# First loads in pieces, idle transposes at the start, reciprocals behind the next maxima

## The chip, the cores and the metric

The kernel runs on one core of one Trainium2 chip. The metric is the device time of the program in microseconds (us), taken as the median of several runs; beside it there is one execution under the hardware profiler, from which every row of the trace comes. The engines are named PE (TensorE), DVE (VectorE), ACT (ScalarE), POOL (GpSimd) and SP (SyncE, which here only issues DMAs). PEld is PE's weight load.

## The reference

Attention with pooled queries, then two feed-forward layers. All data are float32.

```python
q_pool = q.reshape(B, H, S // 2, 2, D).mean(axis=3)      # B 2, H 8, S 1152, D 64
scores = matmul(q_pool, k.T) / sqrt(D)                   # 576 queries x 1152 keys, 16 heads
attn = exp(scores - max(scores))
attn = attn / (sum(attn) + 1e-09)
x = matmul(attn, v)                                      # then (B * 576) x 512
h = x @ w_in;  g = maximum(h, 0) + log1p(exp(-abs(h)));  x = g @ w_out       # 512 -> 2048 -> 512
xn = x / sqrt(mean(x * x) + 1e-06) * rms_g
g = xn @ w_gate;  x = (g / (1 + exp(-g))) * (xn @ w_val) @ w_out2            # 512 -> 1536 -> 512
```

## The kernel before

**Stages.** Attention takes some 290 us, the two feed-forward layers the rest. Attention goes over 8 pairs of heads (`pb`), and within a pair over 4 blocks of 128 queries (`x` 0 to 3) for each head `h`, and a fifth, `x` 4, which holds the last 64 queries of both heads.

**Preparation of a pair (`prep`).** A float32 operand is split into a rounded part and the rest, which PE multiplies one after the other. The keys of both heads come as one tile `kr` (576 KB); for each head `kk` gets the rounded keys on one half of the partitions (a copy, L251 or L253, called at L369) and the rest on the other half (a subtraction, L256, called at L371). The queries come as `qr`, twice for each head (the same 288 KB into either half of the partitions), are summed in pairs into `qs` (L256, called at L353), and scaled and rounded into `qh` (L381 or L383) with the rest in `ql` (L363); 512 columns for the first four blocks, and 64 for the tail. For the first pair the query loads are issued on ACT's queue, all else on SP's. `v` is loaded as it is. `prep(0)` stands first; `prep(1)` follows the first scores; `prep(pb + 1)` is called in block 1 of pair `pb`.

**A block.** `qk` (L400) puts 128 x 1152 scores into PSUM with 6 matmuls (3 for `qh`, 3 for `ql`; 12 in the fifth block). `softmax` takes the negated maximum on DVE (`nm`, L416) and the exponential on ACT (`p`, L418), which also adds up the row sums in `den`. `flip` (L437; `flip_m`, L681, for the fifth block) transposes `p` on PE through two small PSUM banks `t`, with copies to `pt` on ACT or DVE; `av` (L455) multiplies by `v` with 36 matmuls.

**End of a pair.** `scales` works on DVE: add 1e-9 to the 9 columns of `den` (L466), reciprocal (L468), and two copies that repeat it over 64 columns a head (`rdb`, L469 with 512 columns and L472 with 128). `spread` transposes `rdb` on PE (L488) during blocks 1 and 2 of the next pair and multiplies the result of the pair by it.

**The order.** A planner (`Plan`) knows the operations, their engines with estimated durations, and the tiles that they read and write. PE's order is that of the program: in the last block of a pair the transposes, the scores of the next pair's first block (head 1 in block 3, head 0 in block 4), `av`, and then the transposes of the next pair's first block. The order on DVE, ACT, POOL and SP comes out of a list schedule by the latest start that each operation could have; where an operation names two engines, the planner takes one. In its model a POOL operation and a DVE operation that uses the port to SBUF exclude each other in time.

## Time and profile before

| | us |
|---|---|
| time, median of 3 runs (lowest to highest) | 717.67 (717.59 to 718.02) |
| profiled execution: time | 715.96 |
| profiled execution: span from the first to the last instruction | 714.2 |
| busy PE / DVE / ACT / POOL | 681.2 / 447.5 / 334.6 / 100.2 |

The profiled execution's time is 1.76 us longer than its span. Start and end times in rows are microseconds from the start of the span. A wait that a row names is put down to the event that came last.

### The profile page before, as it was taken

The page shows a single profiled execution, that of the slowest core. Times are in us where ns is not written, and L with a number is a line of the kernel's source. Part 1 is how long each engine was busy: PE and PEld are TensorE (multiplying, and loading weights), DVE is VectorE, ACT ScalarE, POOL GpSimd, SP SyncE. Part 2 cuts the span into 40 slices and gives each one's busy share as a digit, 9 for nine tenths or more (in the row PEclk, how much of TensorE's full clock was granted, in tenths as well). Part 3 has the DMA queues.
Part 4 walks back from the last instruction along what each step waited for, and adds up shares of the span by engine and source line. Part 5 has one row for each costly group of instructions (what it writes and reads, how often), then busy time and mean ns, then how long its engine had stood idle before and what let it go on. Part 6 is the DMA issues. An engine that isn't in the chain of part 4 may idle for free.

```text
span 714.2 us, 12314 instructions
## 1 busy us (share of the span) xinstructions
PE 681.2 (95%) x5083; PEld 654.8 (92%) x5083; DVE 447.5 (63%) x755; ACT 334.6 (47%) x609; POOL 100.2 (14%) x75
## 2 busy tenths in 40 slices
PE   1999898989899999999999999999999999999997
PEld 1889898989888898999999999999999999999997
DVE  4778878878686787888534268797877342122222
ACT  2888687777878785544212144454543120010001
POOL 0322424333233022000000000011112000000000
PEclk9999999999999999999999999999999999999999
DMA  7643413343301111553200023352451100010001
GB/s 187 179 123 100 137 57 100 95 127 99 111 20 63 61 60 62 176 177 126 82 1 1 0 64 118 119 171 90 148 178 60 45 0 1 1 45 1 0 1 45
DMA packets 17736, 57.68 MB, mean 81 GB/s; under 512 B 2320, under 2 KB 3856, under 8 KB 17680
## 3 DMA queue, kind: packets, MB, share of 16 engines
q1 hardware_dynamic: 17216, 55.71, 24.6%
q10 hardware_dynamic: 464, 1.18, 0.8%
q8 instruction: 40, 0.66, 0.4%
q14 instruction: 16, 0.13, 0.1%
HBM read 54.53 MB, written 2.36 MB: 80 GB/s over the span
## 4 chain that ended last, share of the span: by engine, by line
PE 88%; DVE 6%; ACT 4%; DMA 1%; issue 1%; ACTq 0%; DVEq 0%
PE s L526 15%; PE s L528 15%; PE s L527 15%; PE s L400 10%; PE t L455 9%; PE t L437 9%; PE t L528 5%; PE t L527 5%; PE t L526 5%; ACT p L418 2%; DVE rdb L469 2%; DVE nm L416 1%; DMA qr<-in_qT_dram 1%; PE t L488 1%; DVE den L466 1%
## 5 line engine op out<-in xcount | busy, mean ns | idle before, releaser
L526 PE MATMUL s<-x,w 128*128 128x384 f32 x348 | 117.8, 338 | 1.3 <-ACT g L647 0.6
L528 PE MATMUL s<-x,w 128*128 128x384 f32 x348 | 116.7, 335 | 0.0
L527 PE MATMUL s<-x,w 128*128 128x384 f32 x348 | 116.6, 335 | 0.0
L416 DVE TENSOR_REDUCE nm<-s 128x1 f32<-128x1152 f32 x72 | 97.1, 1355 | 24.8 <-PE s L400 23.2
L418 ACT ACTIVATE p<-s,nm 128x1152 f32<-128x1152 f32 x72 | 88.1, 1224 | 21.7 <-DVE nm L416 19.7
L437 PE MATMUL t<-ident,p 128*128 128x128 f32 x576 | 82.7, 277 | 11.0 <-ACT p L418 10.8
L251 ACT COPY pt<-t 128x512 f32<-128x512 f32 (+2 forms) x138 | 70.4, 521 | 35.9 <-PE t L437 28.9
L437 PEld LDWEIGHTS t<-ident,p 128*128 128x128 f32 x576 | 65.5, 140 | 21.5 <-ACT p L418 12.7
L647 ACT ACTIVATE g<-s 128x384 f32<-128x384 f32 x36 | 17.7, 491 | 142.7 <-PE s L528 142.7
L526 PE MATMUL s<-gh,w 128*128 128x384 f32 x243 | 81.5, 335 | 0.0
L528 PE MATMUL s<-gh,w 128*128 128x384 f32 x243 | 81.5, 335 | 0.0
L527 PE MATMUL s<-gl,w 128*128 128x384 f32 x243 | 81.4, 335 | 0.0
L455 PE MATMUL t<-pt,v 128*64 128x128 f32 (+1 forms) x1440 | 80.1, 265 | 0.0
L455 PEld LDWEIGHTS t<-pt,v 128*64 128x64 f32 x1440 | 71.3, 137 | 7.3 <-issue 7.3
L526 PEld LDWEIGHTS s<-x,w 128*128 128x128 f32 x348 | 65.4, 188 | 2.8 <-ACT g L647 0.9
L527 PEld LDWEIGHTS s<-x,w 128*128 128x128 f32 x348 | 65.4, 188 | 0.0
L528 PEld LDWEIGHTS s<-x,w 128*128 128x128 f32 x348 | 65.4, 188 | 0.0
L305 ACT ACTIVATE t<-raw 128x512 f32<-128x512 f32 x68 | 45.1, 671 | 21.0 <-DVE w L256 13.4
L256 DVE TENSOR_TENSOR gl<-g,gh 128x384 fp32r<-128x384 f32 x84 | 48.4, 577 | 9.3 <-ACT gh L251 7.1
L253 DVE CAST gh<-g 128x384 fp32r<-128x384 f32 x66 | 26.0, 394 | 43.9 <-PE t L528 41.7
L649 DVE TENSOR_TENSOR g<-g,s 128x384 f32<-128x384 f32 x18 | 9.9, 552 | 62.5 <-ACT g L647 59.3
L315 DVE SCALAR_TENSOR_TENSOR t<-t,t 128x512 int32<-128x512 int32 x68 | 48.0, 705 | 1.7
(129 smaller groups left out, 1208.4 us busy)
## 6 DMA issues: line engine op xcount, KB each, us to landing
raw<-in_w_dram SPq DMA_DIRECT2D x16, 512.0 KB, 3.4
raw<-in_w1o_dram SPq DMA_DIRECT2D x16, 512.0 KB, 3.5
qr<-in_qT_dram SPq DMA_DIRECT2D x28, 288.0 KB, 4.0
raw<-in_wg_dram SPq DMA_DIRECT2D x12, 512.0 KB, 3.5
raw<-in_wv_dram SPq DMA_DIRECT2D x12, 512.0 KB, 3.5
raw<-in_w2o_dram SPq DMA_DIRECT2D x12, 512.0 KB, 3.5
kr<-in_kT_dram SPq DMA_DIRECT2D x8, 576.0 KB, 4.5
v<-in_v_dram SPq DMA_DIRECT2D x16, 288.0 KB, 3.2
```

Of the source, the lines that this page charges most:

```text
L251: nc.scalar.copy(out, in_)
L256: engines[e].tensor_tensor(out=out, in0=in0, in1=in1, op=o)
L305: o = op([("ACT", 0.68)], lambda e: nc.scalar.activation(out=t0(), in_=word(1).bitcast(F32), scale=2.0 ** -112, **(dict(func=AF.Prelu, alp ...
L315: op([dve(DM)], lambda e: nc.vector.scalar_tensor_tensor(out=t0().bitcast(I32), in0=t0().bitcast(I32), scalar=3, in1=t1(), op0=ALU.logical ...
L400: nc.tensor.matmul(sc()[:, c, :N], lhsT=q, rhs=s["kk"][hh]()[:, c * N:(c + 1) * N], start=(hh == heads[0] and z == 0), stop=(hh == heads[- ...
L416: op([dve(S, psum=True)], lambda e: nc.vector.tensor_reduce(out=nm(), in_=sc()[:, :, :N], axis=AX.XY, op=ALU.max, negate=True), r=[(sc, No ...
L418: o = op([("ACT", 1.42)], lambda e: nc.scalar.activation(out=pr(), in_=sc()[:, :, :N], func=AF.Exp, bias=nm(), accum_out=s["den"]()[:, col ...
L437: nc.tensor.transpose(t()[:, i * P:(i + 1) * P], pr[:, c * P:(c + 1) * P], ident)
L455: nc.tensor.matmul(t()[h * D:h * D + D, :n], lhsT=s["v"][h]()[:, c, :], rhs=rhs, start=(c == 0), stop=(c == CK - 1))
L526: nc.tensor.matmul(out, lhsT=w[:, 0, cols], rhs=hi, start=start, stop=False)
L527: nc.tensor.matmul(out, lhsT=w[:, 0, cols], rhs=lo, start=False, stop=False)
L528: nc.tensor.matmul(out, lhsT=w[:, 1, cols], rhs=hi, start=False, stop=stop)
```

## The change

- For the first pair, the queries are loaded in two cuts (the first 128 columns, then the other 448), the first cuts on ACT's queue and the second on SP's; the keys come in three pieces of 384 columns, and the second cuts follow them. Sums, rounding and the rests are made by these pieces, and block 0 of the scores reads the query part `m0`, blocks 1 to 3 `m1`. The second head's sum uses the tile `y` in place of `qs`.
- For the other pairs the sum of the queries is made in two halves and the rest of the keys in three pieces, each on DVE or POOL. The order in which `prep` names its loads and its tail columns changes.
- PE begins with 16 transposes of the identity into a bank that nobody reads.
- `scales` is called after the scores of the next pair's first block, and its first operation is made to depend on the two maxima of that block. The two repeating copies may run on ACT.

```diff
@@ -38,6 +38,7 @@
 SEM = 0.1
 SLACK = 2.0
 WAIT = 5.0
+WARM = 16
 MM = N / 2400 + 0.014
 
 
@@ -339,40 +340,83 @@
     def prep(pb):
         s = st[pb]
         n = 2 * pb
+        first = pb == 0
         s["kk"], s["v"] = [], []
         s["q"] = qx[pb % 2]
         kr = ring("e", "kr", [P, S])
-        load(kr, kT[n:n + 2].rearrange("a d s -> (a d) s"), 576, [(kr, None)])
+        qr, qs = [], []
+        kcuts = [(c, slice(c * N, c * N + N), N) for c in range(KB)]
+        f = NF * P
+        qcuts = ((0, slice(0, P), P), (1, slice(P, SQ), SQ - P))
+
+        def load_q(h, c, cut, m, queue):
+            for z in range(2):
+                load(lambda z=z: qr[h]()[z * D:z * D + D, :, cut], qT[n + h][:, :, cut], m // 2, [(qr[h], (z, c))], queue)
+
         for h in range(2):
-            spare = pb == 0 and h == 1
-            qr = ring("a", "p1", [P, 2, SQ], F32, 2) if spare else ring("e", "qr", [P, 2, SQ])
-            for z in range(2):
-                load(lambda qr=qr, z=z: qr()[z * D:z * D + D], qT[n + h], 288, [(qr, z)], "ACTQ" if pb == 0 else "SP")
-            qs = ring("e", "qs", [P, SQ])
+            qr.append(ring("a", "p1", [P, 2, SQ], F32, 2) if first and h else ring("e", "qr", [P, 2, SQ]))
+            qs.append(ring("a", "y", [P, SQ]) if first and h else ring("e", "qs", [P, SQ]))
+            if first:
+                load_q(h, *qcuts[0], "ACTQ")
+        pairs = kT[n:n + 2].rearrange("a d s -> (a d) s")
+        if first:
+            for c, cut, m in kcuts:
+                load(lambda cut=cut: kr()[:, cut], pairs[:, cut], 192, [(kr, c)])
+        else:
+            load(kr, pairs, 576, [(kr, None)])
+        for h in range(2):
+            if first:
+                load_q(h, *qcuts[1], "SP")
+            else:
+                for z in range(2):
+                    load(lambda h=h, z=z: qr[h]()[z * D:z * D + D], qT[n + h], 288, [(qr[h], (z, 0)), (qr[h], (z, 1))])
+            vt = ring("ea"[pb % 2], f"v{h}{pb % 2}", [P, CK, D])
+            s["v"].append(vt)
+            load(vt, v[n + h], 288, [(vt, None)])
+
+        def round_q(h, key, x, m, i):
             qh, ql = s["q"][h]
-            op([dve(SQ), pool(SQ)], lambda e, qs=qs, qr=qr: tt(e, qs(), qr()[:, 0, :], qr()[:, 1, :], ALU.add),
-               r=[(qr, None)], w=[(qs, None)])
-            f = NF * P
-            c = f if h == 0 else f + D
-            for x, m, src in ((0, f, 0), (c, D, f)):
-                o = slice(x, x + m)
-                i = slice(src, src + m)
-                key = "m" if src == 0 else "e"
-                op([dve(m, True), act(m)], lambda e, qh=qh, qs=qs, o=o, i=i: scale16(e, qh()[:, o], qs()[:, i]),
-                   r=[(qs, None)], w=[(qh, key)])
-                op([dve(m)], lambda e, qh=qh, ql=ql, qs=qs, o=o, i=i: nc.vector.scalar_tensor_tensor(
-                    out=ql()[:, o], in0=qs()[:, i], scalar=0.0625, in1=qh()[:, o], op0=ALU.mult, op1=ALU.subtract),
-                   r=[(qs, None), (qh, key)], w=[(ql, key)])
+            o = slice(x, x + m)
+            op([dve(m, True), act(m)], lambda e: scale16(e, qh()[:, o], qs[h]()[:, i]), r=[(qs[h], None)],
+               w=[(qh, k) for k in key])
+            op([dve(m)], lambda e: nc.vector.scalar_tensor_tensor(
+                out=ql()[:, o], in0=qs[h]()[:, i], scalar=0.0625, in1=qh()[:, o], op0=ALU.mult, op1=ALU.subtract),
+               r=[(qs[h], None)] + [(qh, k) for k in key], w=[(ql, k) for k in key])
+
+        def sum_q(h, cut, m, c):
+            op([dve(m), pool(m)], lambda e: tt(e, qs[h]()[:, cut], qr[h]()[:, 0, cut], qr[h]()[:, 1, cut], ALU.add),
+               r=[(qr[h], (z, x)) for z in range(2) for x in c], w=[(qs[h], c)])
+
+        for h in range(2):
             kk = ring("ea"[pb % 2], f"kk{h}{pb % 2}", [P, S], F32R)
             s["kk"].append(kk)
             hi, lo = slice(h * D, h * D + D), slice(D - h * D, P - h * D)
-            op([act(S)] if pb == 0 else [dve(S, True), act(S)], lambda e, kk=kk, hi=hi: copy(e, kk()[hi], kr()[hi]),
-               r=[(kr, None)], w=[(kk, 0)])
-            op([dve(S), pool(S)], lambda e, kk=kk, hi=hi, lo=lo: tt(e, kk()[lo], kr()[hi], kk()[hi], ALU.subtract),
-               r=[(kr, None), (kk, 0)], w=[(kk, 1)])
-            vt = ring("ea"[pb % 2], f"v{h}{pb % 2}", [P, CK, D])
-            s["v"].append(vt)
-            load(vt, v[n + h], 288, [(vt, None)])
+            if first:
+                c, cut, m = qcuts[0]
+                sum_q(h, cut, m, (0,))
+                round_q(h, ("m0",), 0, P, slice(0, P))
+                for c, cut, m in kcuts:
+                    op([dve(m, True), act(m)], lambda e, kk=kk, hi=hi, cut=cut: copy(e, kk()[hi, cut], kr()[hi, cut]),
+                       r=[(kr, c)], w=[(kk, ("h", c))])
+                    op([dve(m)], lambda e, kk=kk, hi=hi, lo=lo, cut=cut: tt(
+                        e, kk()[lo, cut], kr()[hi, cut], kk()[hi, cut], ALU.subtract),
+                       r=[(kr, c), (kk, ("h", c))], w=[(kk, ("l", c))])
+            else:
+                for cut in (slice(0, SQ // 2), slice(SQ // 2, SQ)):
+                    sum_q(h, cut, SQ // 2, (0, 1))
+                round_q(h, ("m0", "m1"), 0, f, slice(0, f))
+                op([dve(S, True), act(S)], lambda e, kk=kk, hi=hi: copy(e, kk()[hi], kr()[hi]),
+                   r=[(kr, None)], w=[(kk, ("h", c)) for c in range(KB)])
+                for c, cut, m in kcuts:
+                    op([dve(m), pool(m)], lambda e, kk=kk, hi=hi, lo=lo, cut=cut: tt(
+                        e, kk()[lo, cut], kr()[hi, cut], kk()[hi, cut], ALU.subtract),
+                       r=[(kr, None), (kk, ("h", c))], w=[(kk, ("l", c))])
+        for h in range(2):
+            if first:
+                c, cut, m = qcuts[1]
+                sum_q(h, cut, m, (1,))
+                round_q(h, ("m1",), P, f - P, slice(P, f))
+            round_q(h, ("e",), f if h == 0 else f + D, D, slice(f, SQ))
         s["den"] = ring("a", "den", [P, 2 * NF + 1], F32, 2)
         s["O"] = ring("a", "O", [P, SQ], F32, 2)
 
@@ -401,7 +445,7 @@
                                      start=(hh == heads[0] and z == 0), stop=(hh == heads[-1] and z == 1))
         r = []
         for hh, z in todo:
-            r += [(s["kk"][hh], None), (s["q"][hh][z], "m" if x < NF else "e")]
+            r += [(s["kk"][hh], None), (s["q"][hh][z], "m0" if x == 0 else "m1" if x < NF else "e")]
             if x == NF:
                 r.append((s["q"][hh][z], "z"))
         op([("PE", 0.09 + MM * KB * len(todo))], go, r=r, w=[(sc, None)])
@@ -413,7 +457,7 @@
         nm = ring("a", f"nm{h}", [P, 1], F32, 2)
         pr = u["p"] = ring("a", f"p{h}", [P, KB, N], F32, 2)
         col = 2 * NF if x == NF else h * NF + x
-        op([dve(S, psum=True)], lambda e: nc.vector.tensor_reduce(out=nm(), in_=sc()[:, :, :N], axis=AX.XY, op=ALU.max, negate=True),
+        u["mx"] = op([dve(S, psum=True)], lambda e: nc.vector.tensor_reduce(out=nm(), in_=sc()[:, :, :N], axis=AX.XY, op=ALU.max, negate=True),
            r=[(sc, None)], w=[(nm, None)])
         o = op([("ACT", 1.42)], lambda e: nc.scalar.activation(out=pr(), in_=sc()[:, :, :N], func=AF.Exp, bias=nm(),
                                                           accum_out=s["den"]()[:, col:col + 1]),
@@ -462,15 +506,17 @@
     def scales(pb):
         s = st[pb]
         den = s["den"]
+        behind = [units[pb + 1, 0, h]["mx"] for h in range(2) if (pb + 1, 0, h) in units]
         rd = s["rd"] = ring("a", "rdb", [P, NF + 1, 2, D])
-        op([("DVE", 0.17, 1)], lambda e: nc.vector.tensor_scalar(out=den(), in0=den(), scalar1=1e-9, scalar2=None, op0=ALU.add),
-           w=[(den, None)])
+        o = op([("DVE", 0.17, 1)], lambda e: nc.vector.tensor_scalar(out=den(), in0=den(), scalar1=1e-9, scalar2=None,
+                                                                    op0=ALU.add), w=[(den, None)])
+        o.deps.update(behind)
         op([("DVE", 0.25, 1)], lambda e: nc.vector.reciprocal(den(), den()), w=[(den, None)])
-        op([dve(NF * P)], lambda e: nc.vector.tensor_copy(
-            rd()[:, :NF], den()[:, :2 * NF].rearrange("p (h x) -> p x h", h=2).unsqueeze(3).to_broadcast([P, NF, 2, D])),
+        op([dve(NF * P), act(NF * P)], lambda e: copy(
+            e, rd()[:, :NF], den()[:, :2 * NF].rearrange("p (h x) -> p x h", h=2).unsqueeze(3).to_broadcast([P, NF, 2, D])),
            r=[(den, None)], w=[(rd, 0)])
-        op([dve(P)], lambda e: nc.vector.tensor_copy(
-            rd()[:, NF], den()[:, 2 * NF:].unsqueeze(2).to_broadcast([P, 2, D])),
+        op([dve(P), act(P)], lambda e: copy(
+            e, rd()[:, NF], den()[:, 2 * NF:].unsqueeze(2).to_broadcast([P, 2, D])),
            r=[(den, None)], w=[(rd, 1)])
 
     def spread(pb, part):
@@ -693,6 +739,12 @@
             fed[0] += 1
 
     prep(0)
+    warm = tbank()
+
+    def heat(e):
+        for _ in range(WARM):
+            nc.tensor.transpose(warm()[:, :P], ident, ident)
+    op([("PE", 4.0)], heat, w=[(warm, None)])
     qk(0, 0, 0)
     qk(0, 0, 1)
     prep(1)
@@ -720,7 +772,6 @@
                     qk(pb + 1, 0, 1)
                 T[4]()
             else:
-                scales(pb)
                 T[0]()
                 T[1]()
                 if not last:
@@ -728,6 +779,7 @@
                 else:
                     make_banks(1, "h")
                     m1_h(0)
+                scales(pb)
                 T[2]()
                 av(*prev)
             prev = (pb, x)
```

## Rows read from the trace of the kernel before

**Rows 1.** The page's busy time by engine: us, share, instructions.

```profile
PE 681.2 (95%) x5083; PEld 654.8 (92%) x5083; DVE 447.5 (63%) x755; ACT 334.6 (47%) x609; POOL 100.2 (14%) x75
```

**Rows 2.** Waits of PE over the span: us in total, times, longest.

```profile
PE s L400 <- DVE kk L256: 14.1, 2, 13.9
PE t L437 <- ACT p L418: 10.8, 8, 1.8
```

**Rows 3.** Stage window: length, busy us (instructions) by engine, PEclk, DMA share, GB/s.

```profile
23.00:290.00 267.00, 256.00 (x2645) 233.34 (x2644) 210.38 (x297) 202.47 (x363) 82.24 (x55) 1.00 0.30 93
```

**Rows 4.** Timeline of PE: start, length, instructions [idle before <- releaser].

```profile
21.92 1.13 PE L437 MATMUL t<-ident,p 128*128 128x128 f32 x8 [0.76 <-ACT p L418]
49.58 0.66 PE L437 MATMUL t<-ident,p 128*128 128x128 f32 x4 [0.65 <-ACT p L418]
82.58 0.66 PE L437 MATMUL t<-ident,p 128*128 128x128 f32 x4 [1.78 <-ACT p L418]
...
246.34 0.66 PE L437 MATMUL t<-ident,p 128*128 128x128 f32 x4 [0.57 <-ACT p L418]
```

**Rows 5.** Timeline of all engines at the second change of pairs.

```profile
74.10 1.41 POOL L256 TENSOR_TENSOR qs<-qr 128x576 f32<-128x576 f32 x1 [7.27 <-PE t L455]
...
74.33 1.21 DVE L466 TENSOR_SCALAR den<-den 128x9 f32<-128x9 f32 x1
...
75.59 2.67 POOL L256 TENSOR_TENSOR kk<-kr,kk 64x1152 fp32r<-64x1152 f32 x1
...
75.83 2.72 DVE L469 COPY rdb<-den 128x512 f32<-128x512 f32 x1
...
78.47 2.61 DVE L416 TENSOR_REDUCE nm<-s 128x1 f32<-128x1152 f32 x2
```

**Rows 6.** Timeline of all engines at the seventh change of pairs.

```profile
240.74 0.42 DVE L469 COPY rdb<-den 128x512 f32<-128x512 f32 x1
...
243.58 1.36 DVE L416 TENSOR_REDUCE nm<-s 128x1 f32<-128x1152 f32 x1 [0.80 <-PE s L400]
...
244.97 1.22 ACT L418 ACTIVATE p<-s,nm 128x1152 f32<-128x1152 f32 x1 [0.50 <-DVE nm L416]
```

**Rows 7.** Chain that ended last, in order of time: start, us, what.

```profile
1.74 8.65 DMA qr<-in_qT_dram
...
23.05 1.06 PE s L400 x6
```

**Rows 8.** Timeline of all engines at the start.

```profile
1.01 0.29 POOL masks.py:199 TENSOR_SCALAR_AFFINE_SELECT ident<-ident 128x128 f32<-128x128 f32 x1
...
5.03 2.32 ACT L251 CAST kk<-kr 64x1152 fp32r<-64x1152 f32 x2 [3.02 <-DMA kr<-in_kT_dram]
...
12.47 1.35 DVE L256 TENSOR_TENSOR kk<-kr,kk 64x1152 fp32r<-64x1152 f32 x1
...
13.87 1.33 PE L400 MATMUL s<-kk,qhA 128*128 128x384 f32 x3 [13.87 <-DVE kk L256]
...
15.00 1.16 PE L400 MATMUL s<-kk,qlA 128*128 128x384 f32 x3
```

**Rows 9.** Windows of the first loads, columns as in rows 3.

```profile
2.00:5.00 3.00, 0.00 (x0) 0.00 (x0) 0.06 (x1) 0.01 (x1) 0.00 (x0) 1.00 0.86 316
5.00:11.00 6.00, 0.00 (x0) 0.00 (x0) 0.51 (x1) 2.30 (x2) 0.00 (x0) 1.00 1.05 214
```

**Rows 10.** DMA queue of ACT (q10), 0 to 12 us: packets, MB, share of 16 engines.

```profile
q10 hardware_dynamic: 460, 1.18, 45.1%
```

**Rows 11.** Groups by shape, 0 to 290 us: count | busy us, mean ns | idle before.

```profile
L256 DVE TENSOR_TENSOR kk<-kr,kk 64x1152 fp32r<-64x1152 f32 x3 | 4.1, 1353 | 0.1
...
L256 DVE TENSOR_TENSOR qs<-qr 128x576 f32<-128x576 f32 x4 | 3.0, 759 | 8.5 <-DMA qr<-in_qT_dram 8.4
...
L256 POOL TENSOR_TENSOR kk<-kr,kk 64x1152 fp32r<-64x1152 f32 x13 | 34.5, 2651 | 63.7 <-ACT kk L251 63.3
...
L256 POOL TENSOR_TENSOR qs<-qr 128x576 f32<-128x576 f32 x11 | 15.5, 1411 | 56.7 <-PE t L455 29.0 <-DVE qlB L363 20.2 <-DVE qlA L363 7.4
```

## The prediction

> **What bounds the kernel now.** First the page: PE is busy for 681.2 of 714.2 us [rows 1], so everything that is to be won lies in the 33 us in which it is not, and the next view is what PE waits for. Two entries hold nearly all of it [rows 2]: 14.1 us for the rest of the keys (13.9 of them before the first matmul) and 10.8 us in eight waits for the exponential. In the stage of attention from 23 us on PE is busy for 256.0 of 267.0 us [rows 3]: the 11 us that are missing are those waits again, so between them PE sets the pace and DVE (210 of 267) has room. The timeline of PE then gives each wait its place [rows 4]: one at 21.92 us (0.76), while the first block gets going, and one at each of the seven changes of pairs, of 0.65 (first), 1.78 (second) and 0.57 (seventh), with four more like the second; those five together are 10.8 - 0.76 - 0.65 - 0.57 = 8.82 us. What lies between two waits is bound by PE and untouched by the change. So the sum has two terms: what the start gives and what the changes of pairs give.
>
> **The changes of pairs.** At the second one DVE wants to add 1e-9 to nine numbers at 74.33 us, which takes 1.21 us, and to copy 512 columns at 75.83 us, which takes 2.72 us [rows 5]. The same copy takes 0.42 us at the seventh change [rows 6]. The difference is POOL: its subtraction of the keys starts at 75.59 and ends at 78.26, its sum of the queries ends at 75.51 [rows 5], and both DVE operations end only some 0.3 us after the POOL operation that they met (the copy) or 0.03 us after it (the addition). They wait for the whole POOL operation. Behind the copy stand both maxima of the next pair's first block, 2.61 us back to back from 78.47 us [rows 5], then head 0's exponential, then the transposes that PE waits for. At the seventh change no POOL operation is in the way and only head 0's own maximum is left to do when its scores end: maximum at 243.58, exponential at 244.97, transposes at 246.34 [rows 6, 4], and PE still waits 0.57 us, because what it has to do meanwhile (av) is shorter than a maximum and an exponential. That is the floor.
>
> With `scales` behind both maxima nothing that waits for POOL stands ahead of them by construction, and head 1's maximum, whose scores PE makes first, is done when head 0's scores end, as at the seventh change. Each of the five waits falls from 1.76 to 0.57 us: 8.82 - 5 x 0.57 = 5.97 us, and the first from 0.65 to 0.57: 0.08 us. The seventh stays. Together 6.05 us. Bounds: nothing, if something else takes the copy's place in the queue, and 10.04 us (all seven gone), which the seventh change excludes, since it has the same chain without the stall. I take 6.05.
>
> The four operations of `scales` now run beside the exponentials, when DVE has little that PE waits for; behind them stand the copies of `av` and of the first transposes, and those follow PE's wait by less than the stall would now be: with pieces of 384 columns a POOL operation takes, on the line through 1411 ns at 576 and 2651 ns at 1152 columns [rows 11], some 1.0 us and not 2.65. `rdb` itself is next needed in block 1 of the next pair, behind a whole block of PE work, so its own lateness costs nothing. If that cover failed, a late copy would cost PE at most the 1.0 us at each change.
>
> **Smaller pieces.** On DVE the line through 759 and 1353 ns [rows 11] has a fixed part of 0.165 us, on POOL of 0.17 us. A pair (33.0 us from change to change, rows 4) has one more sum and two more subtractions for each head, 6 x 0.17 = 1.0 us, at most 1.0 us on DVE, whose idle time in attention is (267 - 210) / 8 = 7 us a pair [rows 3]. I take nothing. The bounds are 0 and 7 us (1 us for each of seven pairs, all on the path).
>
> **The start.** Now: the first queries land 8.65 us after their issue, at 10.39 [rows 7], though the keys were there at 5.03 us, when ACT starts to round them [rows 8]; then sum, rounding and subtraction of full width on DVE, the subtraction alone from 12.47 for 1.35 us; the first matmul at 13.87 [rows 8]; and PE is dense from 21.92 us on [rows 4], when the second head's exponential is there. I carry the start as the shift of that moment.
>
> Landing: the keys and the four first cuts are 590 + 262 = 852 KB. From 2 to 5 us the DMA engines moved 316 GB/s, from 5 to 11 us 214 GB/s [rows 9]. By bytes at the first rate they are in at 2.0 + 2.7 = 4.7 us. By packets it is later: a packet of the query loads cost 0.451 x 16 x 12 / 460 = 188 ns of an engine [rows 10], at some 2.6 KB; the change makes runs of 512 bytes (512 of them) and of 1,536 bytes (384), and if each cost as much, that is 896 x 0.188 / 16 = 10.5 us, so 12.5 us. A shorter packet should be nearer to its bytes; I take 6.0 us. Behind that the last piece of keys is rounded in about 0.4 us (a third of 1.16, rows 8) and subtracted in 0.165 + 384 x 1.03 ns = 0.56 us: first matmul at some 7.1 us.
>
> From then on DVE decides. It has, by the same line, two sums of 128 columns (0.6), their two rests (0.6), six subtractions of keys (3.4), the second cut of head 0, which block 1 needs ahead of head 1's transposes on PE (sum and rest of 448 columns, 1.25), and two maxima (2.7): 8.5 us from the first landed queries at some 4.5 us, with 0.8 us of waiting for keys: 13.8 us, and with the exponential of 1.22 us [rows 6] 15.1 us. Against 21.92 that is 6.8 us earlier. Bounds: with the packets at full price the last keys land at 12.5, the first matmul comes at 13.6, and there is no shift worth the name; with half the price they land at 7.3, with the second cuts behind them, and the shift is some 4 us; with data at 4.7 us and DVE not in the way it is 10 us. Head 1's second cut comes next on DVE (1.25 us), then block 1's maximum; by the same count its exponential is ready about when PE is, so no new wait of more than some 0.5 us.
>
> Against pieces in a load the Trainium skill, "DMA: Bandwidth & Descriptors", section "Rules for kernel authors", says to put many small transfers together, since one under 64 KB is mostly overhead; its table of bandwidths has 0.95 us of engine time for 64 KB. The first cuts are 64 KB each here; by that figure, as an estimate, the four cuts take 3.8 us and the keys some 3 us more, so that the last key lands at some 9 us and the start gives some 4 us. No row shows a transfer of that size.
>
> **The idle transposes.** Eight transposes take 1.13 us when PE is fast [rows 4]. The first six matmuls took 2.29 us [rows 8], six later 1.06 us [rows 7], a ratio of 2.2, near that of PE's two levels (1.2 and 2.4 GHz), though the clock column reads 1.00 throughout. Sixteen transposes from some 1.4 us, when the identity is there (POOL ends it at 1.30, rows 8), take 2.3 us at the fast and some 5 us at the slow level, so to 3.7 or 6.4 us: covered by the wait for the keys (7.1 us). If the keys came at 5.8 they would cost 0.6 us. If PE is fast afterwards, the first scores end 1.2 us earlier, but DVE is busy then; I take nothing, and 1.2 us either way for the range.
>
> **Sum.** 6.05 + 6.8 = 12.85 us. The profiled execution goes from 715.96 to 703.1 us, its span from 714.2 to 701.3. The median of the runs lies 1.7 us above the profiled execution, and I leave that as it is: 704.8 us.
>
> **Rivals.**
> - *The pieces land no sooner.* The 64-partition query loads moved 214 GB/s with the engines full [rows 9]; shorter runs may fill them with less. With packets between half and full price (shifts of 4 and 0 us) the start gives 2 us: 717.7 - 6.05 - 2 = 709.6. It speaks against it that the keys, first in line, landed at 5.03 [rows 8], when 3 x 316 = 948 KB had moved [rows 9], 360 KB of them other data. Half the price alone (4 us) makes 707.6, the milder form. The page's rule above would do about that.
> - *A new operation takes the copy's place.* The schedule is made anew; the time of DVE that `scales` leaves free ahead of the maxima can be filled by a fast copy or an addition that meets a POOL piece, of up to 1.0 us. Each of five waits keeps about 1 us of its 1.2: 717.7 - 6.8 - 1 = 709.9. Against it: a piece holds DVE for 1.0 and not 2.7 us, and head 1's maximum has 1 us to spare.
> - *DVE becomes the bound of attention.* 13 of 16 key subtractions run on POOL now [rows 11]; in pieces the planner may give them to DVE, at 3 x 0.56 x 2 = 3.4 us a pair, with 1.0 us for the pieces and 1 more for unlucky waits: some 5 of its 7 idle us. Seven pairs hold 31 us of that; from 40% of it on PE's path the gain of 12.85 is gone, and at 60% the time is 724. The room of 7 us and the planner's own count of DVE speak against it.
> - *The change does nothing*, if the waits at the changes are set elsewhere and the first key tile, not the queries, was late: 717.7. The chain from the query load to the first matmul [rows 7, 8] is against it.
>
> **How the numbers follow.** The forecast has 0.65, with a range of its own of 700.5 to 708 us; the landing rival 0.15, of which 0.05 for the milder form; the new wait 0.12; DVE as the bound 0.05; nothing 0.03. Time within 0.2% (1.4 us) is what a measurement of this kernel cannot tell from no change. All but the last two are faster by more: 0.92 faster, 0.03 same, 0.05 slower. The range takes in the forecast's range and the first two rivals: 700.3 to 710.3 us, and leaves out 0.08 for the last two and some 0.06 for sizes beyond the bounds.
>
> **What would show it.** Right: the first score matmul at some 7 us, PE dense from some 15 us; waits at the changes of pairs of about 0.6 us, with additions and copies of `scales` behind both maxima; POOL operations of 1.0 us at most on keys; PE busy by 2 to 5 us more for the idle transposes. Wrong: keys or first cuts that land after 8 us; a DVE operation of over 1 us just ahead of a maximum; new waits of PE for copies to `pt` or for the second cuts in the first 30 us; a larger wait at the last block.

## The result and the profile after

| | before | after |
|---|---|---|
| time, median of 4 runs each (lowest to highest) | 717.63 us (716.13 to 718.02) | 708.76 us (708.23 to 709.5) |
| profiled execution: time | 715.96 | 708.70 |
| profiled execution: span | 714.2 | 706.9 |

The ratio is 0.9881 with a 95% interval of 0.9864 to 0.9898: 8.9 us faster, where 12.85 us were forecast. The time lies inside the stated range (700.3 to 710.3 us), but above the 700.5 to 708 us that the prediction gave to its forecast alone: it lies in the part that the rivals had added. Line numbers have moved: the scores are L444 (before: L400), the transposes L481, the subtractions L257.

The page's busy time by engine answers to [rows 1]:

```profile
PE 687.4 (97%) x5099; PEld 659.6 (93%) x5099; DVE 437.6 (62%) x763; ACT 336.0 (48%) x620; POOL 106.6 (15%) x112
```

PE's busy time rose by 6.2 us, 3.55 of them the idle transposes, while the span fell by 7.3 us. The waits of PE (us in total, times, longest) answer to [rows 2]:

```profile
PE s L444 <- DVE kk L257: 6.4, 4, 3.8
PE t L481 <- ACT p L462: 4.1, 7, 0.6
```

The seven waits at the changes of pairs have come down to 4.1 us, and the wait for keys from 14.1 to 6.4. The timeline of PE says where they stand, and answers to [rows 4]:

```profile
1.36 3.55 PE L746 MATMUL t<-ident 128*128 128x128 f32 x16 [1.36 <-POOL ident masks.py:199]
8.71 0.66 PE L444 MATMUL s<-kk,qhA 128*128 128x384 f32 x1 [3.80 <-DVE kk L257]
...
11.42 0.69 PE L444 MATMUL s<-kk,qhA 128*128 128x384 f32 x1 [0.22 <-DVE kk L257]
...
20.50 0.78 PE L444 MATMUL s<-kk,qhB 128*128 128x384 f32 x3
...
79.31 0.66 PE L481 MATMUL t<-ident,p 128*128 128x128 f32 x4 [0.57 <-ACT p L462]
```

The second change waits 0.57 us, and so do all the others but one (0.64). The first score matmul is at 8.71 us, but the other pieces of keys come later, the last at 11.42 us. The row at 20.50 us, where the second head's scores of block 1 begin, serves below as the mark for the start: PE is dense from it on. In the profiled execution before, the same scores begin at 22.81 us (row under e11), so against that execution the start has moved by 2.3 us and not by 6.8.

The timeline of all engines around the first loads answers to [rows 8]:

```profile
3.29 0.35 DVE L254 CAST kk<-kr 64x384 fp32r<-64x384 f32 x1 [1.22 <-DMA kr<-in_kT_dram]
...
7.70 0.29 DVE L257 TENSOR_TENSOR qs<-qr 128x128 f32<-128x128 f32 x1 [4.06 <-DMA qr<-in_qT_dram]
8.02 0.55 DVE L257 TENSOR_TENSOR kk<-kr,kk 64x384 fp32r<-64x384 f32 x1
...
8.35 1.58 ACT L252 CAST kk<-kr 64x384 fp32r<-64x384 f32 x3
8.53 1.14 POOL L257 TENSOR_TENSOR qs<-qr 128x448 f32<-128x448 f32 x1 [7.22 <-DMA qr<-in_qT_dram]
8.60 1.27 DVE L254 CAST kk<-kr 64x384 fp32r<-64x384 f32 x1
```

The first key piece is rounded at 3.29 us. Then DVE stands still for 4.06 us at the sum of the first query cut, which lands only at 7.70, and the subtraction of that key piece, ready since 3.64 us, stands behind it (8.02); so do three more key copies on ACT, behind the rounding of the queries (8.35). When POOL starts the sum of the second cut at 8.53, the key copy that DVE starts at 8.60 takes 1.27 us and not 0.35.

The DMA view of 2 to 8 us (the queue's packets, MB and share of 16 engines, then issues with the median us to landing) says why the cut was late, beside [rows 10]:

```profile
q10 hardware_dynamic: 707, 0.26, 21.7%
...
kr<-in_kT_dram SPq DMA_DIRECT2D x1, 192.0 KB, 5.2
...
qr<-in_qT_dram ACTq DMA_DIRECT2D x1, 64.0 KB, 5.8
```

The loads of 64 KB for head 0 need 5.8 us to land (the one in this window; the median of both is 5.6), the third piece of keys 5.2. The bytes of the first cuts are not what held them up: ACT's whole queue used 0.217 x 6 = 1.3 us of the 16 engines' time, 0.217 x 16 x 6 / 707 = 29 ns for a packet of some 370 bytes on average, against 188 ns for one of 2.6 KB before. The average takes in small packets of another load (2 KB, on the same queue); shared among the 512 runs of 512 bytes alone, the whole time would be 41 ns for each.

The windows of the start answer to [rows 3, 9], with the granted clock after the five busy times:

```profile
1.00:5.00 4.00, 3.55 (x16) 3.28 (x16) 1.39 (x9) 1.52 (x2) 0.29 (x1) 1.00 0.69 199
...
8.70:13.70 5.00, 3.62 (x8) 2.34 (x8) 4.48 (x8) 1.90 (x5) 0.96 (x1) 0.50 1.02 279
13.70:18.20 4.50, 3.23 (x12) 3.09 (x12) 4.05 (x7) 2.81 (x7) 0.00 (x0) 0.50 0.62 186
```

PE idles from 4.9 to 8.7 us, after the last idle transpose, and the granted clock is 0.50 from 8.7 to 18.2 us, the level of 1.2 GHz. Under the idle transposes the column reads 1.00, though the sixteen took 3.55 us, where at the rate of 1.13 us for eight [rows 4] they would take 2.3: some of them ran slowly.

At the second change of pairs the timeline of all engines answers to [rows 5]:

```profile
74.15 1.36 DVE L460 TENSOR_REDUCE nm<-s 128x1 f32<-128x1152 f32 x1 [0.35 <-PE s L444]
...
74.88 4.20 POOL L257 TENSOR_TENSOR kk<-kr,kk 64x384 fp32r<-64x384 f32 x4
...
75.43 0.74 DVE L427 TENSOR_SCALAR qhB<-qs 128x512 fp32r<-128x512 f32 x1
...
76.55 1.36 DVE L460 TENSOR_REDUCE nm<-s 128x1 f32<-128x1152 f32 x1 [0.38 <-PE s L444]
...
77.83 0.32 DVE L511 TENSOR_SCALAR den<-den 128x9 f32<-128x9 f32 x1
...
78.43 1.07 DVE L254 COPY rdb<-den 128x512 f32<-128x512 f32 x2
```

Four POOL pieces run back to back from 74.88 to 79.08 us. A DVE copy, rounding or addition that meets one now waits for that piece alone: rounding 512 queries takes 0.74 us here, where the kernel before has 0.42 at 29.61 us, the addition 0.32 and the two copies of `rdb` 1.07 together. The maxima start at 74.15 and 76.55 us, as soon as their scores are done.

### The profile page after: what moved, and what is told of

It reads as the page before. It is cut to its first block, busy times and chain, and to the rows that moved or that the text cites. A ratio compares the mean times of both kernels' runs of the same rounds, so it can differ in the third digit from the quotient of the medians.

```text
span 706.9 us, 12426 instructions
## 1 busy us (share of the span) xinstructions
PE 687.4 (97%) x5099; PEld 659.6 (93%) x5099; DVE 437.6 (62%) x763; ACT 336.0 (48%) x620; POOL 106.6 (15%) x112
## 4 chain that ended last, share of the span: by engine, by line
PE 92%; DVE 4%; ACT 2%; DMA 1%; issue 1%; ACTq 0%; DVEq 0%
PE s L572 15%; PE s L574 15%; PE s L573 15%; PE s L444 12%; PE t L481 10%; PE t L499 9%; PE t L574 5%; PE t L572 5%; PE t L573 5%; DVE nm L460 1%; PE t L727 1%; ACT p L462 1%; PE t L534 1%; DMA qr<-in_qT_dram 1%; DVE t L314 0%
## 5 line engine op out<-in xcount | busy, mean ns | idle before, releaser
L252 ACT COPY pt<-t 128x512 f32<-128x512 f32 (+1 forms) x140 | 72.3, 524 | 35.6 <-PE t L481 27.9
L481 PE MATMUL t<-ident,p 128*128 128x128 f32 x576 | 83.6, 279 | 4.6 <-ACT p L462 4.1
L693 ACT ACTIVATE g<-s 128x384 f32<-128x384 f32 x36 | 17.7, 491 | 143.7 <-PE s L574 143.7
L481 PEld LDWEIGHTS t<-ident,p 128*128 128x128 f32 x576 | 65.9, 141 | 15.4 <-ACT p L462 6.0
L257 DVE TENSOR_TENSOR gl<-g,gh 128x384 fp32r<-128x384 f32 x83 | 47.1, 568 | 8.5 <-ACT gh L252 6.4
L254 DVE CAST gh<-g 128x384 fp32r<-128x384 f32 x61 | 23.8, 390 | 42.3 <-PE t L574 40.9
L594 ACT ACTIVATE g<-s 128x384 f32<-128x384 f32 x36 | 17.7, 492 | 67.1 <-PE s L574 59.5
```

The costliest lines, as they stand in the source:

```text
L252: nc.scalar.copy(out, in_)
L254: engines[e].tensor_copy(out, in_)
L257: engines[e].tensor_tensor(out=out, in0=in0, in1=in1, op=o)
L481: nc.tensor.transpose(t()[:, i * P:(i + 1) * P], pr[:, c * P:(c + 1) * P], ident)
```

## Experiments

Each kernel was timed in turns with the kernel before on the same chip, whose median there was 716.95 us (e1 to e4), 717.02 (e5 to e8) and 717.28 (e9 to e11). A gain is the difference to that median; that of the changed kernel, which was timed ahead of these, is 8.9 us. The intervals reach up to 1 us to either side, so that smaller differences between rows of different groups say little.

| kernel | time, us | gain, us | ratio, 95% interval | mark, us |
|---|---|---|---|---|
| changed kernel | 708.76 | 8.9 | 0.9864 to 0.9898 | 20.50 |
| e1: move of scales alone | 714.87 | 2.1 | 0.9961 to 0.9982 | 23.50 |
| e5: small pieces alone | 712.48 | 4.5 | 0.9923 to 0.9950 | 23.97 |
| e2: changed, scales not moved | 708.21 | 8.7 | 0.9867 to 0.9894 | 20.27 |
| e3: changed, no idle transposes | 708.80 | 8.2 | 0.9875 to 0.9902 | 20.96 |
| e4: changed, 44 idle transposes | 707.86 | 9.1 | 0.9862 to 0.9889 | 20.06 |
| e6: changed, first sums on DVE | 708.22 | 8.8 | 0.9866 to 0.9897 | 20.77 |
| e7: changed, first cuts on SP | 705.34 | 11.7 | 0.9828 to 0.9855 | 17.49 |
| e8: changed, keys ahead on DVE | 708.15 | 8.9 | 0.9861 to 0.9898 | 20.06 |
| e9: e7 with 34 idle transposes | 703.68 | 13.6 | 0.9800 to 0.9827 | 16.21 |
| e10: e9, scales not moved | 703.67 | 13.6 | 0.9797 to 0.9824 | 16.06 |

**e1, the move of `scales` alone** (the new `scales` with its dependence on the maxima, its copies on DVE or ACT and its new place, in the kernel before).

```diff
+        behind = [units[pb + 1, 0, h]["mx"] for h in range(2) if (pb + 1, 0, h) in units]
...
+        o.deps.update(behind)
...
-                scales(pb)
                 T[0]()
                 T[1]()
...
+                scales(pb)
                 T[2]()
```

> The kernel before with the move of scales alone (behind both maxima, copies on DVE or ACT); loads and POOL operations stay whole. Theory A, the move alone ends the stall: PE waits 0.57 us at every change of pairs and the time falls by some 6.0 us, to 711.6 us. Rival B, the small POOL pieces are needed too: the addition and the copy still meet a whole POOL operation of 1.4 or 2.7 us, now behind the maxima, and hold up the copies that PE needs next, so that 2 us or less are won (715.6 us or more).

2.1 us, and 714.87 us: nearer to rival B, just below its 715.6. The timeline at its second change:

```profile
80.83 1.35 DVE L256 TENSOR_TENSOR kk<-kr,kk 64x1152 fp32r<-64x1152 f32 x1
...
82.10 1.35 DVE L416 TENSOR_REDUCE nm<-s 128x1 f32<-128x1152 f32 x1
...
84.85 0.66 PE L437 MATMUL t<-ident,p 128*128 128x128 f32 x4 [0.83 <-ACT p L418]
```

`scales` no longer stands ahead of the maxima, and PE's wait falls from 1.78 to 0.83 us, as it does at the third to sixth changes. It does not fall to 0.57, because the planner now has the whole subtraction of keys on DVE (80.83, 1.35 us) between the two maxima; head 0's maximum starts at 82.10 and not at 81.8, when its scores are done. At the first change the same kernel shows what a whole POOL operation does behind the maxima:

```profile
49.78 2.63 POOL L256 TENSOR_TENSOR kk<-kr,kk 64x1152 fp32r<-64x1152 f32 x1
50.01 2.42 DVE L467 TENSOR_SCALAR den<-den 128x9 f32<-128x9 f32 x1
...
53.97 0.28 DVE L253 COPY O<-t 128x128 f32<-128x128 f32 x1
...
54.30 0.66 PE L437 MATMUL t<-ident,p 128*128 128x128 f32 x4 [1.09 <-DVE O L253]
```

The addition to nine numbers waits 2.42 us for the POOL operation of 2.63 us, the copy of `av`'s result out of PSUM comes at 53.97, and PE waits 1.09 us for it, a wait that the kernel before does not have. Another new one, of 1.14 us at 46.98 us, is a wait for a copy to `pt` on ACT, which stands there behind the rounding of a whole key tile (1.15 us), with no POOL operation in it. So the move takes 10.0 us of waits at the seven changes down to 5.4, and gives 2.2 us back in these two places.

**e5, the small pieces alone** (in the kernel before, for all pairs but the first).

```diff
-            op([dve(SQ), pool(SQ)], lambda e, qs=qs, qr=qr: tt(e, qs(), qr()[:, 0, :], qr()[:, 1, :], ALU.add),
...
+            for i in ((slice(0, SQ),) if pb == 0 else (slice(0, SQ // 2), slice(SQ // 2, SQ))):
...
-            op([dve(S), pool(S)], lambda e, kk=kk, hi=hi, lo=lo: tt(e, kk()[lo], kr()[hi], kk()[hi], ALU.subtract),
...
+            for i in ((slice(0, S),) if pb == 0 else [slice(c * N, c * N + N) for c in range(KB)]):
+                m = i.stop - i.start
+                op([dve(m), pool(m)], lambda e, kk=kk, hi=hi, lo=lo, i=i: tt(e, kk()[lo, i], kr()[hi, i], kk()[hi, i], ALU.subtract),
```

> The kernel before with the sums of the queries in halves and the subtractions of the keys in three pieces for all pairs but the first, and nothing else. Theory G, the small POOL pieces are what ends the stall: PE waits about 0.57 us at the changes of pairs and the time falls by 5 to 6 us, to 711 to 712 us (before: 717.0 here). Rival H, the gain of the changes needs the other parts too: as with the move of scales alone, 2 us or less (715 us or more).

4.5 us, a little under theory G's 5 to 6 and far from rival H: six of the seven waits are 0.57 us; the first is 1.37. The timeline at its second change:

```profile
82.58 0.84 DVE L473 COPY rdb<-den 128x512 f32<-128x512 f32 x1
...
83.82 0.66 PE L441 MATMUL t<-ident,p 128*128 128x128 f32 x4 [0.57 <-ACT p L422]
```

`scales` is called at its old place, but the planner made the order anew with the smaller pieces: the addition still stands ahead of the maxima (76.75 us, 0.59), while the copy of `rdb` that took 2.72 us ahead of them before now comes behind both (79.18 and 81.06 us). This holds for the second to sixth changes. So e5 has the small pieces and, unasked, the copies behind the maxima too.

**e2, the changed kernel with `scales` at its old place** (the first diff backwards).

> The changed kernel with scales at its old place, in front of the maxima and on DVE: start and small pieces alone. Theory A, the move is what ends the stall: the waits at the changes stay at 1.2 to 1.8 us and the time is 712.5 to 715 us. Rival B, the pieces alone do most of it, since a DVE operation now waits for 1.0 us of POOL and not for 2.7: waits of 0.6 to 0.8 us and 708.7 to 710 us.

8.7 us: as fast as the changed kernel, and 0.5 us under rival B's range. The timeline at its second change:

```profile
71.67 0.59 DVE L510 TENSOR_SCALAR den<-den 128x9 f32<-128x9 f32 x1
...
73.06 6.12 POOL L257 TENSOR_TENSOR kk<-kr,kk 64x384 fp32r<-64x384 f32 x6
...
76.01 1.36 DVE L460 TENSOR_REDUCE nm<-s 128x1 f32<-128x1152 f32 x1 [0.54 <-PE s L444]
...
77.52 0.81 DVE L513 COPY rdb<-den 128x512 f32<-128x512 f32 x1
...
78.77 0.66 PE L481 MATMUL t<-ident,p 128*128 128x128 f32 x4 [0.57 <-ACT p L462]
```

The addition stands ahead of the maxima again, meets a POOL half of a sum and takes 0.59 us; the maximum of head 0 starts at 76.01, right behind its scores, and PE waits 0.57 us. The reciprocal and the copies come after the maxima even without the dependence, since the planner put them there (77.52). So with small pieces the named dependence and the new place of the call are worth nothing that can be told. What the pieces would give with the copies ahead of the maxima is not shown: in e2, e5 and e10 the planner has moved them at the second to sixth changes.

**e3 and e4, no idle transposes, and 44 of them** (`WARM`, with the planner's order kept).

```diff
-WARM = 16
+WARM = 0
```

> The changed kernel without the 16 idle transposes, all else in the same order. Theory C, they do nothing, since the granted clock was back at 0.50 when the first scores came (8.7 us, after 3.8 us of idle PE): 708.3 to 709.3 us. Rival D, they still shorten the slow stretch: 1 us or more slower without them, 709.8 us or more.

> The changed kernel with 44 idle transposes in place of 16, which should last until about 8.7 us, all else in the same order. Theory E, the half clock from 8.7 to 18.2 us is on the path: PE stays at 1.00, the six matmuls of a first block take 1.1 and not 2.3 us, and the time falls by 1.5 to 2.5 us, to 706.3 to 707.3 us. Rival F, DVE's queue alone sets the start: less than 0.5 us is won (708.3 us or more).

Without them the time is that of the changed kernel (theory C; by the gains 0.7 us apart, which says little). With 44 it is 0.9 us shorter than without, between the two expectations. The windows of e4 show why so little:

```profile
5.00:8.70 3.70, 3.20 (x28) 2.86 (x26) 1.22 (x4) 0.94 (x3) 0.00 (x0) 1.00 0.81 179
8.70:13.70 5.00, 2.63 (x8) 1.63 (x7) 4.79 (x8) 1.62 (x4) 1.35 (x1) 0.77 1.05 281
13.70:18.20 4.50, 3.91 (x14) 3.78 (x15) 3.65 (x7) 3.50 (x7) 0.00 (x0) 0.50 0.75 234
```

The clock holds at 1.00 under the transposes, but then PE waits for keys between its first matmuls, the mean of the next 5 us is 0.77, and from 13.7 us on the clock is at 0.50.

**e6, the first pair's sums on DVE alone.**

```diff
-            op([dve(m), pool(m)], lambda e: tt(e, qs[h]()[:, cut], qr[h]()[:, 0, cut], qr[h]()[:, 1, cut], ALU.add),
+            op([dve(m)] if first else [dve(m), pool(m)], lambda e: tt(e, qs[h]()[:, cut], qr[h]()[:, 0, cut], qr[h]()[:, 1, cut], ALU.add),
```

> The changed kernel with the first pair's sums on DVE alone, so that POOL has nothing to do at the start. Theory I, the POOL sum of 1.14 us that held the rounding copy on DVE for 0.9 us is on the path of the start: 0.6 to 0.9 us are won (707.9 to 708.2 us), though DVE gets the sum of 0.6 us in exchange only later. Rival J, it takes from DVE as much as it gives: 708.5 us or more.

No gain that the measurement can tell (708.22, 707.3 to 709.05), and a mark of 20.77 us. The key copy takes 0.35 us and the block's last key piece meets PE at 10.84 us instead of 11.42, but DVE pays with the sum later, as rival J says. In its profile the first cut also landed 0.34 us later, so the two can't be told apart cleanly.

**e7, the first cuts of the queries on SP's queue.**

```diff
-                load_q(h, *qcuts[0], "ACTQ")
+                load_q(h, *qcuts[0], "SP")
```

> The changed kernel with the first cuts of the queries on SP's queue, behind the keys and ahead of the second cuts, in place of ACT's. Theory K, the first cuts came late (7.7 us) because the second cuts on the other queue shared the DMA engines with them: they land by 6 us, the first score matmul comes by 7 us, and 2 to 3 us are won (705.7 to 706.7 us). Rival L, 512-byte runs are slow wherever they stand: they land after 7 us again, and less than 1 us is won.

2.8 us more than the changed kernel wins, at 705.34 us a little under theory K's range, though the first score matmul is at 7.41 and not by 7 us. The issues with the us to landing, and the timeline of all engines:

```profile
qr<-in_qT_dram SPq DMA_DIRECT2D x2, 64.0 KB, 3.1
p<-in_qT_dram SPq DMA_DIRECT2D x2, 64.0 KB, 2.5
```

```profile
6.80 0.29 DVE L257 TENSOR_TENSOR qs<-qr 128x128 f32<-128x128 f32 x1
...
7.41 0.80 PE L444 MATMUL s<-kk,qhA 128*128 128x384 f32 x3 [2.50 <-DVE qhA L427]
```

The same 512-byte runs land 3.1 and 2.5 us after their issue, where they took 5.6 and 5.2 beside the second cuts on another queue; the third key piece lands in 3.6 us and not 5.2. DVE's wait for the first cut is gone, because the planner, told that the cuts come after the keys, put the key work first; the first block's matmuls run in one go from 7.41 us.

**e8, the key work ahead of the first sum on DVE, loads unchanged.**

```diff
-                sum_q(h, cut, m, (0,))
+                sums.append(sum_q(h, cut, m, (0,)))
...
+                    sums[0].deps.add(o)
```

> The changed kernel with the first sum of the queries made to depend on all six subtractions of the first pair's keys, so that they stand ahead of it on DVE; the loads as they are. Theory M, the key work queued on DVE and ACT behind the sum that waits for the first cut sets the start: with that work done by 7.7 us the six matmuls of the first block run in one go from about 8.7 us and 2 to 3.5 us are won (705.3 to 706.8 us). Rival N, the half clock or the second cuts set the start: less than 1 us is won.

708.15 us: theory M fell, and the time is within rival N's bound. The timeline of all engines:

```profile
6.37 0.35 DVE L254 CAST kk<-kr 64x384 fp32r<-64x384 f32 x1 [1.15 <-DMA kr<-in_kT_dram]
6.76 2.08 DVE L257 TENSOR_TENSOR kk<-kr,kk 64x384 fp32r<-64x384 f32 x4
...
8.87 0.29 DVE L257 TENSOR_TENSOR qs<-qr 128x128 f32<-128x128 f32 x1
...
9.48 1.33 PE L446 MATMUL s<-kk,qhA 128*128 128x384 f32 x3 [4.45 <-DVE qhA L429]
```

The third key piece, which shares the engines with the first and second cuts, lands at 6.37, and the sum that stood in the way before now comes at 8.87, behind four subtractions. The six matmuls run in one go, but from 9.48 us and at the slow clock, and the mark comes only 0.4 us earlier. The first cut did not hold the sum up here: issued at some 1.8 us at the latest, and 5.5 us at most to land, it was there by 7.3 us. Three of the six subtractions are for the second head, which the first block does not need. So this order wins nothing while the keys are late; what a sum behind head 0's three alone would give was not run.

**e9 and e10, e7 with 34 idle transposes, and that with `scales` at its old place.**

```diff
-WARM = 16
+WARM = 34
```

> The kernel of e7_first_sp (first cuts on SP's queue behind the keys, 705.3 us) with 34 idle transposes in place of 16, which should last to about 7.3 us, just before the first score matmul at 7.4. Theory E, the half clock is on the path once the data come early enough: the granted clock stays at 1.00 through the first blocks and 1.5 to 2.5 us are won (702.8 to 703.8 us). Rival F, as in e4_long_idle PE is too sparsely busy after the first scores and falls back: 0 to 1 us (704.3 us or more).

> The kernel of e9_sp_long with scales at its old place. Theory G, with small POOL pieces the move of scales is worth nothing: within 0.6 us of e9_sp_long, waits of 0.57 us at the changes. Rival A, the move gives some of it: 1 us or more slower than e9_sp_long.

1.9 us more than e7 (theory E; in the profiled executions the mark comes 1.3 us earlier), and no difference between the two (theory G). The windows of e9:

```profile
6.50:8.70 2.20, 2.16 (x16) 1.82 (x14) 2.04 (x6) 0.00 (x0) 0.00 (x0) 1.00 1.01 253
8.70:13.70 5.00, 3.46 (x20) 2.56 (x19) 4.85 (x8) 2.95 (x8) 1.14 (x1) 1.00 1.03 271
13.70:18.20 4.50, 3.54 (x27) 3.04 (x26) 3.95 (x7) 3.57 (x7) 1.13 (x2) 1.00 0.95 297
```

Now PE goes from the last idle transpose (done at 7.57 us) to the first scores (7.61) without a gap, and the clock stays at 1.00, though later scores wait 0.27 and 1.04 us. Both beat the kernel before by 13.6 us, and the changed one by 13.6 - 8.9 = 4.7.

**e11, the kernel before, profiled once more.**

> The kernel before, unchanged, profiled once more. Theory O, its profiled execution of 715.96 us was shorter than the median because PE's clock rose early in it (first fast matmuls at 18.3 us): another execution of some 717 us shows the same schedule with the slow matmuls lasting to 20 us or more. Rival P, the difference is spread over the whole run (matmuls longer by a fraction of a per cent).

This execution took 717.61 us. The timeline of PE:

```profile
18.34 1.33 PE L400 MATMUL s<-kk,qlB 128*128 128x384 f32 x3 [0.63 <-DVE qlB L363]
...
20.17 1.31 PE L400 MATMUL s<-kk,qhA 128*128 128x384 f32 x3
...
24.34 0.77 PE L400 MATMUL s<-kk,qhB 128*128 128x384 f32 x3
```

The other execution of the same kernel had:

```profile
18.34 0.79 PE L400 MATMUL s<-kk,qlB 128*128 128x384 f32 x3 [0.75 <-DVE qlB L363]
...
22.81 0.77 PE L400 MATMUL s<-kk,qhB 128*128 128x384 f32 x3
```

Theory O: the first four groups of three matmuls begin at the same times in both (13.88, 15.00, 16.41 and 18.34 us here), but the fourth takes 1.33 us and not 0.79, the groups behind it are slow too (1.31 us at 20.17), and the mark stands at 24.34 and not at 22.81, 1.5 of the 1.6 us between the two spans. Against this execution, which is nearer to the median, the changed kernel's start has moved by 24.34 - 20.50 = 3.8 us. The marks of e1 and e5, which leave the first loads as they were, are 23.50 and 23.97: over the four executions with the old start the shift is 2.3 to 3.8 us.

## Why the prediction was right, and where not

**What bounds the kernel** held: PE sets the pace of attention, and the gain is what its waits lost. Between the mark and the last short wait of attention (L437 at 273.68 us in e11, L481 at 264.08 us after) the changed kernel is 5.8 us shorter, the start gives 3.8, and the two feed-forward layers took 0.7 us longer in that execution; together 8.9.

**Changes of pairs**: 6.05 us were forecast and the waits gave 5.9 (10.0 us in e11, 4.1 after), less a new wait of 0.35 us for a copy to `pt`. The floor of 0.57 us, read off the seventh change, is what stands at six of the seven. The mechanism (DVE waits for the whole POOL operation that it met, and the maxima stand behind the copy) was right. What was wrong is how the 6 us were put down: all of them to the move of `scales`, and "nothing" to the smaller pieces. e1 shows that the move alone takes 4.6 us off these waits, leaves 0.83 us at five of them, since a whole subtraction on DVE steps between the maxima, gives 2.2 us back at the first change and wins 2.1. e5 shows that the pieces alone win 4.5, and e2 and e10 that beside them the named move adds nothing that can be told. The two do not add up because they meet in one thing: in e5, e2 and e10 the planner itself put the copies behind the maxima. How much of the 4.5 us is the shorter wait for POOL and how much that order was not parted. So the size came out right by luck in part: the prediction had not counted on the pieces, and the move without them falls 4 us short.

**The start** is the term that was mis-sized: 6.8 us against 2.3 to 3.8. One of the prediction's own signs of being wrong was there: the last of head 1's first cuts, issued at 3.8 us, landed after 8 us. The size itself was within reach: with the loads in line and a fast PE the mark of e9 is at 16.21 us, 6.6 us ahead of 22.81. Four things stood behind the shortfall.
- "A shorter packet should be nearer to its bytes" was right, but "I take 6.0 us" for the landing was not: head 0's first cuts were there only at 7.70 us, because the second cuts were issued on the other queue from 2.11 us on and shared the DMA engines with them. e7, where they land 2.5 to 3.1 us after their issue, speaks for it. The prediction had the second cuts behind the first, which they are not when they are on another queue. The Trainium skill, "DMA: Bandwidth & Descriptors", section "Queues, rings and completion order", says that each engine takes turns between its queues packet by packet; e7 agrees. By the figure that the prediction cited from the Trainium skill, "DMA: Bandwidth & Descriptors", which stands there in the table of section "Bandwidth" for loads issued from GpSimd, the four cuts would be, as an estimate, 3.8 us of engine time; the trace shows 1.3 for these, issued from ACT.
- The first sum stood ahead of the key work on DVE and ACT, so 4.06 us of waiting held up work that was ready, where 0.8 us had been allowed for. e8, with all six subtractions first, won nothing, but held the sum back itself, so that it does not price a better order; with the cuts on SP's queue wait and order fall together, and the runs do not part them further.
- The POOL sum of the second cut cost a key copy 0.9 us. e6 could not show that in the time.
- "I take nothing, and 1.2 us either way" for a fast PE afterwards held for the changed kernel, where PE was not fast afterwards: the 16 transposes do nothing that can be told (e3), not because DVE hides their gain, but because the clock had fallen again by the first scores. With the data late a longer row of them is worth 0.9 us (e4); with the data earlier 1.9 us (e9 against e7), more than the 1.2.

**The reference of the start** was itself off: the profiled execution before had its clock rise early, and 21.92 us was not typical (e11). The 1.7 us between that execution and the median, which the prediction carried over without a cause, are mostly this: 1.5 us of them lie ahead of the mark.

**The rivals**: DVE did not become the bound; it is busy for 204.1 us from 23 to 290 us, less than the 210.4 of before [rows 3]. No new operation ahead of the maxima kept a wait in the changed kernel; in e1 the subtraction between them did (0.83 us). Late landing was the rival nearest to what happened, by another cause than packet prices.

Open: why the clock of two executions of one program rises at different times, how much of e7's gain is the load and how much the order that the planner made for it, and, likewise for e5, how much is the shorter POOL operation and how much the planner's order.

## What to carry to other kernels

When operations of a fast engine end only with the whole operation of a slower one that they met, try to cut the slow operation too, and not only to move the fast ones: here the cut alone won 4.5 us, and the move alone 2.1, since it gave half of what it took off the waits back elsewhere. Where a planner makes the order, read from the trace what it moved by itself before you say which edit did it. Loads that are needed first should not share the DMA engines with loads that are needed later: here it helped to put them in line on one queue; a second queue gave them no priority. Idle matmuls were worth most here (1.9 us) when the real ones followed without a gap, 0.9 with short waits behind them and nothing that can be told with 3.8 us of idle PE, so look at the granted clock after them and not only during them.

## What the runs showed of the hardware

- A packet took 29 ns of a DMA engine at 370 bytes on average (at most 41 ns for a run of 512 bytes) and 188 ns at 2.6 KB in these windows: short runs cost about the same per byte here. 64 KB landed 2.5 to 3.1 us after issue in e7, in line on one queue, and 5.2 to 5.8 in the changed kernel, with later loads on another.
- Additions, copies and roundings of DVE that met an operation of POOL ended about when it did: an addition to 128x9 numbers took 0.16 us alone (239.31 us in the kernel before), 1.21 us [rows 5] and 2.42 us (e1) behind whole POOL operations, and 0.32 us in the changed kernel. The maxima took 1.36 us beside POOL too (76.55 us in the changed kernel).
- The granted clock went from 1.00 to 0.50 while PE idled for 3.8 us behind the transposes of the changed kernel, and stayed there for 9.5 us of interrupted work. In e4 it fell after PE had waited 0.50, 0.46 and 1.28 us between its first matmuls; in e9, whose first scores followed the transposes without a gap, it did not fall.
- The clock column of the kernel before reads 1.00 from the start, though its first score matmuls (18 in e11) ran slowly, 1.12 us from one group of three to the next against 0.61 later: at the start of these executions the column can't be trusted, and the durations decide.
